# Row maxima gathered early, one weight's tiles spread over a stage, VectorE work queued behind the maxima

## The chip, the cores and the metric

The kernel runs on one core of one Trainium2 chip. The core has a matrix engine (TensorE, PE in the profile), VectorE (DVE), ScalarE (ACT), GpSimd (POOL) and DMA queues, here all issued by SyncE (SP). Each engine works through its own instruction queue in order; semaphores hold an instruction back until what it needs is there. The metric is the device time of one execution in microseconds, the median of several runs.

## The reference

Three blocks in a row, on 2 batches of 448 tokens with 768 channels:

```python
x = attention(q, k, v)                       # 12 heads of 64, causal
# mixer: over tokens, then over channels
h = np.maximum(x.transpose(0, 2, 1) @ w_tok1, 0.0) @ w_tok2
u = x + h.transpose(0, 2, 1)
y = u + np.maximum(u @ w_ch1, 0.0) @ w_ch2   # 768 -> 1536 -> 768
# gated block
h = gelu_tanh(y @ w_in)                      # 768 -> 2 x 512
a, v = h[..., :512], h[..., 512:]
v_n = (v - mean(v)) / np.sqrt(var(v) + 1e-06) * g_ln
v_s = np.einsum('ts,bsd->btd', w_sg, v_n) + b_sg[None, :, None]
out = y + (a * v_s) @ w_out                  # 512 -> 768
```

Inputs are float32 but the weights come as 64-bit words and are turned into float32 on the chip.

## The kernel before

Everything is kept with channels on the partitions (128 rows) and tokens along the row. After attention and the token mixer come these stages, named by their PSUM tiles:

- r (`channel_up`): u times `w_ch1` in 12 tiles of 128 channels.
- y (`channel_down`): 12 tiles `y_ps`, six channel tiles `m` by two batches `b`, 36 matmuls each. Each `m` needs two tiles of `w_ch2` of 128x768, one for each half of the contraction.
- v: seven token tiles `v_ps` of y times the second half of `w_in` (`w_inv`, in `wv32`), 18 matmuls each; token tile 3 has tokens of both batches and reads them from `y3`, into which POOL copies 64 columns of each y tile.
- ug: y times the first half of `w_in` (`w_inu`, four tiles of 128x768), then g (the mixing of tokens with `w_sg`, and the product `ug`), then o (twelve tiles times `w_out`, added to y by the `ob` instruction and written out).

A weight tile takes the same way everywhere (`decode`): SP loads 768 KB of raw words into `wraw` (two buffers), ACT turns the high words into a float (L117), DVE shifts (L120) and joins in the low words (L121). For the y stage `load_w` then splits it into two float32r parts: ACT casts `whi` (L130), POOL subtracts `wlo` (L99), three buffers each. For v, ug, g and o the operands are split into two float16 parts, scaled by the largest value of the tile. That maximum is found in steps: `absmax` makes row maxima (`yam`, `wvam`, `wam`, `gtam`), a reduction makes one column of them, PE spreads this column over all partitions with a matmul against the identity (`ys_ps`, `w_ps`, `gt_ps`), DVE reduces the result and takes the reciprocal (`spread`), and `split16` makes the high part on ACT and the low part on DVE (`y16`, `wl`). `to16` does it for y of one batch, `begin16` and `end16` for a tile of `w_inu` or `w_out`, `gate16` for the product.

The code states what depends on what. In which order the instructions stand in each engine's queue is set by a scheduler that simulates the program with its own costs; `tc.issue_after(x)` tells it to put instructions behind x.

Of the kernel before, what the change touches and what calls it, by code (L numbers as in the profile page):

```python
# [9 lines left out]
BF16 = mybir.dt.bfloat16  # L10
F16 = mybir.dt.float16
F32 = mybir.dt.float32
# [3 lines left out]
ALU = mybir.AluOpType  # L16
# [8 lines left out]
TOP = 32768.0  # L25
# [3 lines left out]
def mixer_kernel(  # L29
# [37 lines left out]

    const = ctx.enter_context(tc.tile_pool(name="const", bufs=1))
    wpool = ctx.enter_context(tc.tile_pool(name="wpool", bufs=2))
    stp16 = ctx.enter_context(tc.tile_pool(name="stp16", bufs=2))  # L70
    sc = ctx.enter_context(tc.tile_pool(name="sc", bufs=1))
    upool = ctx.enter_context(tc.tile_pool(name="upool", bufs=1))
    rs = ExitStack()
# [66 lines left out]

    def absmax(dst, src):

        nc.vector.tensor_reduce(dst, src, AX.XY if len(src.shape) == 3 else AX.X, ALU.max, apply_absolute_value=True)

    def spread(pm, cols, inv, s, top):

        am = stp16.tile([P, 1], BF16, tag="am16", name="am16")
        nc.vector.tensor_reduce(am, cols, AX.X, ALU.max)
        nc.tensor.matmul(pm[:, :P], am.to_broadcast([P, P]), ident_b, start=True, stop=True)
        nc.vector.reduce_max(inv, pm[:, :P], axis=AX.X)  # L150
        nc.vector.tensor_scalar(inv, inv, 1e-20, 1.0 / top, ALU.max, ALU.mult)
        nc.vector.reciprocal(s, inv)
# [44 lines left out]
    def channel_up(m, batches, pool, psum):  # L197

        wh, wl = load_w(w_ch1[m])
        for b in batches:  # L200
# [6 lines left out]
            nc.vector.scalar_tensor_tensor(rl, pr[:, :S], 0.0, f32(rh), ALU.max, ALU.subtract)  # L207
            r_of[m, b] = (rh, rl)

    def channel_down(m, ws, batches, psum, tmp):  # L210

        for b in batches:
            py = psum.tile([P, 512], F32, tag="d", name="y_ps")
            mm3(py[:, :S], [((ws[c // NCC][0][:, c % NCC, :], ws[c // NCC][1][:, c % NCC, :]), r_of[c, b]) for c in range(NFF)])
            t = tmp.tile([P, S], F32, tag="yt", name="yt")
            nc.vector.tensor_add(t, py[:, :S], f32(u_hi[m][b]))  # L216
            y32[m][b] = upool.tile([P, S], F32, tag=f"uh{m}_{b}", name=f"y{m}_{b}")
            nc.gpsimd.tensor_add(y32[m][b], t, f32(u_lo[m][b]))  # L218
            absmax(yam[:, b, m:m + 1], y32[m][b])

    with ExitStack() as at:
        tokw = at.enter_context(tc.tile_pool(name="tokw", bufs=1))
# [280 lines left out]
    with rs:  # L503
        ps_d = ctx.enter_context(tc.tile_pool(name="ps_d", bufs=8, space=PSUM, reuse_waits="tile"))
        r1pool = rs.enter_context(tc.tile_pool(name="r1pool", bufs=1, reuse_waits="tile"))
        tmp = rs.enter_context(tc.tile_pool(name="tmp", bufs=3, reuse_waits="tile"))
        for m in range(NFF):
            channel_up(m, [1] if m < NF0 else [0, 1], r1pool, ps_d)
        def pst(name):
            return ps_d.tile([P, 512], F32, tag="d", name=name)  # L510

        def to16(b):

            spread(pst("ys_ps"), yam[:, b], *ysc[b], TOP)
            nc.vector.tensor_mul(vinv[:, 2 * b:2 * b + 1], ysc[b][0], wvsc[0])
            hs = slice(64 * b, 64 * b + 64)
            nc.vector.tensor_copy(vinv[hs, 1:2], vinv[hs, 2 * b:2 * b + 1])
            for m in range(NCC):
                y16[m][b] = upool.tile([P, 2, S], F16, tag=f"ul{m}_{b}", name=f"y16_{m}_{b}")
                split16(y16[m][b][:, 0], y16[m][b][:, 1], y32[m][b], ysc[b][1][:, 0:1])  # L520
                ts = slice((1 - b) * (S - 64), (1 - b) * (S - 64) + 64)
                nc.gpsimd.tensor_copy(y3[:, :, m, 64 * b:64 * b + 64], y16[m][b][:, :, ts])

        ws = {}
        for m in range(NCC):
            ws[m] = [
                load_w(w_ch2[m, :, c:c + NCC, :], **(dict(pool=tmp, bufs=1) if (m, c) == (NCC - 1, NCC) else {}))
                for c in (0, NCC)
            ]
            channel_down(m, ws[m], range(B) if m < NCC - 2 else [0], ps_d, tmp)  # L530
            for c in range(2 * m, 2 * m + 2) if m < NCC // 2 else ():
                decode(wv32[:, c, :], w_inv[:, c, :])
                absmax(wvam[:, c:c + 1], wv32[:, c, :])
            if m == NCC // 2:
                spread(pst("wv_ps"), wvam, *wvsc, TOP)
            for c in range(2 * m - NCC, 2 * m - NCC + 2) if m >= NCC // 2 else ():
                split16(wvh[:, c, :], wvl[:, c, :], wv32[:, c, :], wvsc[1][:, 0:1])
        channel_down(NCC - 2, ws[NCC - 2], [1], ps_d, tmp)
        to16(0)
        channel_down(NCC - 1, ws[NCC - 1], [1], ps_d, tmp)  # L540

    def ytok(i, c, vt):
        o = vt * P - S if vt > 3 else vt * P
# [28 lines left out]
    def begin16(src, j):  # L572

        k = src.shape[1]
        m = wpool.tile([P, WC], F32, tag="wm", name="wm", bufs=3)[:, :k * P]
        decode(m, src.rearrange("p a f -> p (a f)"))
        am = gw.tile([P, 1], F32, tag="wam", name="wam")
        absmax(am, m)
        begun.append((j, k, m, am))

# [10 lines left out]
    for vt in range(NV):  # L591
        if vt == 1:
            to16(1)
        if vt > 2:
            end16()
        if 2 <= vt <= 5:
            begin16(w_inu[vt - 2], vt - 2)
        pv = pst("v_ps")
        mm3(pv, [((ytok(0, c, vt), ytok(1, c, vt)), (wvh[:, c, :], wvl[:, c, :])) for c in range(NCC)])
        vg = gw.tile([P, DH], F32, tag="vg", name="vg")  # L600
        si = 0 if vt < 3 else 1 if vt == 3 else 2
        nc.scalar.activation(vg, pv, AF.Gelu_apprx_tanh, scale=vinv[:, si:si + 1])
        st = gw.tile([P, 6], F32, tag="st", name="st")
        nc.vector.bn_stats(st, vg)
        nc.vector.bn_aggr(mv[:, vt, :], st)
        rs = gw.tile([P, 1], F32, tag="rs", name="rs")
        nc.vector.tensor_scalar(rs, mv[:, vt, 1:2], 1.0e-6, ZSCALE ** -2, ALU.add, ALU.mult)
        nc.gpsimd.tensor_tensor(rs, rs, nhalf, ALU.pow)
        nc.vector.tensor_scalar(vg, vg, mv[:, vt, 0:1], rs[:, 0:1], ALU.subtract, ALU.mult)
        if vt != 3:  # L610
            nc.gpsimd.tensor_scalar(z_hi[:, vt, :], vg, 1.0, 0.0, ALU.mult, ALU.add)
            nc.gpsimd.tensor_sub(z_lo[:, vt, :], vg, z_hi[:, vt, :])
            continue
        for b in range(B):
            hs, ls = (slice(64 * i, 64 * i + 64) for i in (b, 1 - b))
            nc.scalar.copy(zz[b][hs], vg[hs])
            nc.gpsimd.tensor_sub(zz[b][ls], vg[hs], zz[b][hs])
# [33 lines left out]
    def gate16(b):  # L651

        us = slice(b * S, (b + 1) * S)
        spread(pst("gt_ps"), gtam[:, b], *gtsc[b], TOP)
        nc.vector.tensor_scalar(oinv[:, b], winv[:, NDC:], gtsc[b][0][:, 0:1], None, ALU.mult)
        for m in range(NDC):
            split16(gt_hi[:, m, us], gt_lo[:, m, us], ug[:, m, us], gtsc[b][1][:, 0:1])

    for b in range(B):
        us = slice(b * S, (b + 1) * S)  # L660
        for m in range(NDC):
            if b == 0 and m < 2:
                end16()
            if b == 1 and m == 2:
                gate16(0)
            ds_ = slice(m * P, (m + 1) * P)
            pg = pst("g_ps")
            nc.tensor.matmul(pg[:, :S], zz[b][:, ds_], sgh[:, 3, :], start=True, stop=False)
            nc.tensor.matmul(pg[:, :S], zz[b][:, ds_], sgl[:, 3, :], start=False, stop=False)
            vts_ = [c + 4 * b for c in range(3)]  # L670
            mm3(pg[:, :S], [((z_hi[:, vt, ds_], z_lo[:, vt, ds_]), (sgh[:, c, :], sgl[:, c, :])) for c, vt in enumerate(vts_)], True)
            gt = gw.tile([P, S], F32, tag="gt", name="gt")
            nc.vector.scalar_tensor_tensor(gt, pg[:, :S], gcol[:, m:m + 1], bb, ALU.mult, ALU.add)
            for cs, ts in rotated(b):
                nc.vector.tensor_mul(ug[:, m, cs], gt[:, ts], ug[:, m, cs])
            absmax(gtam[:, b, m:m + 1], ug[:, m, us])
    for b in range(B):
        us = slice(b * S, (b + 1) * S)
        for m in range(NCC):
            wh, wl = w16[NDC + m]  # L680
            if b == 0 and m == 2:
                gate16(1)
            ob = gw.tile([P, S], F32, tag="ob", name="ob")
            po = pst("o_ps")
            mm3(po[:, :S], [((wh[:, c, :], wl[:, c, :]), (gt_hi[:, c, us], gt_lo[:, c, us])) for c in range(NDC)])
            nc.vector.scalar_tensor_tensor(ob, po[:, :S], oinv[:, b, m:m + 1], y32[m][b], ALU.mult, ALU.add)
            nc.sync.dma_start(out[b, m], ob)


# [51 lines left out]
```

## Time and profile before

| | |
|---|---|
| runs | 427.32, 428.35, 430.29 us, median 428.35 |
| profiled execution | 431.07 us |
| its span | 429.3 us (1.8 us lie around it) |
| TensorE busy | 396.7 us (92%) |
| VectorE busy | 281.1 us (65%) |
| GpSimd busy | 205.1 us (48%) |
| ScalarE busy | 204.2 us (48%) |
| TensorE waits behind 196 us | 2.6 for `y_ps`, 1.3 for `ys_ps`, 1.4 for `w_ps`, 1.6 for `gt_ps` |

The rows below are read so: a timeline gives the start of an instruction in us from the span's start, its duration, engine, line, operation, what it writes and reads, and in brackets how long the engine had been idle before it and what released it. An instruction's duration reaches a little into the next one's. With xN, N instructions that followed each other stand in one row. A table of windows gives the busy time of each engine in a stretch, the clock granted to TensorE as a part of full speed, and the busy share of the DMA engines.

### The profile page before, as it was taken

What the parts mean: (1) busy time and instruction counts of PE and PEld (TensorE: products, weight loads), DVE (VectorE), ACT (ScalarE), POOL (GpSimd) and SP (SyncE); (2) the same over time, 40 slices, a digit from 0 to 9 for tenths busy, and PEclk for the clock granted to TensorE, in tenths of its full rate; (3) what the DMA queues carried; (4) which work ended last, traced back from release to release, by engine and by line L of the source; (5) the groups of instructions that cost most, each with busy time, mean ns of one, the idle gap of its engine ahead of it and who ended that gap; (6) DMA issues with size and microseconds to landing.
All of it is one profiled execution on the core that took longest, in us unless ns stands there. A gap on an engine that the chain in (4) does not pass through costs nothing.

```text
span 429.3 us, 7145 instructions
## 1 busy us (share of the span) xinstructions
PE 396.7 (92%) x2602; PEld 304.8 (71%) x2602; DVE 281.1 (65%) x661; ACT 204.2 (48%) x384; POOL 205.1 (48%) x205
## 2 busy tenths in 40 slices
PE   5778899796899999999999979999998989999896
PEld 3445687674688999999999969999983435555453
DVE  4979665799735745454545363359568999679822
ACT  3789767578866454454344222234143544432200
POOL 3686847678877572655124066364243847100000
PEclk9999899999999999999999989999999999999999
DMA  7899878999955835455536443344122022100122
GB/s 212 186 291 244 184 131 181 241 261 283 237 131 125 199 121 171 143 204 168 159 121 206 152 151 101 120 147 144 53 32 78 0 99 98 49 2 0 66 105 87
DMA packets 61458, 60.98 MB, mean 142 GB/s; under 512 B 47856, under 2 KB 53104, under 8 KB 61424
## 3 DMA queue, kind: packets, MB, share of 16 engines
q1 hardware_dynamic: 61424, 60.54, 52.2%
q8 instruction: 20, 0.33, 0.3%
q14 instruction: 14, 0.11, 0.1%
HBM read 46.50 MB, written 2.75 MB: 115 GB/s over the span
## 4 chain that ended last, share of the span: by engine, by line
PE 49%; DMA 17%; DVE 12%; issue 7%; POOL 7%; ACT 5%; SPq 3%; POOLq 0%; ACTq 0%; DVEq 0%
DMA wraw<-in 8%; PE y_ps L165 5%; PE y_ps L163 5%; PE y_ps L164 5%; DMA vr<-in 4%; PE r_ps L165 4%; PE r_ps L164 4%; PE r_ps L163 4%; DMA pT<-hl 3%; POOL wlo L99 2%; PE ug_ps L163 2%; PE ug_ps L164 2%; PE ug_ps L165 2%; PE o_ps L163 2%; PE o_ps L165 2%
## 5 line engine op out<-in xcount | busy, mean ns | idle before, releaser
L99 POOL TENSOR_TENSOR wlo<-wm,whi 128x768 fp32r<-128x768 f32 x31 | 66.3, 2138 | 57.6 <-ACT whi L130 55.1
L117 ACT ACTIVATE wm<-wraw 128x768 f32<-128x768 f32 (+2 forms) x47 | 38.8, 825 | 64.8 <-POOL wlo L99 45.5
L338 POOL TENSOR_TENSOR hl<-pe,hl 128x512 f16<-128x512 f32 x43 | 54.6, 1277 | 26.4 <-ACT hl L337 25.0
L311 PE MATMUL s_ps<-k,q 128*128 128x64 f32 (+3 forms) x216 | 55.0, 393 | 9.2 <-DMA q<-in 4.4
L120 DVE TENSOR_SCALAR wm<-wm 128x768 int32<-128x768 int32 (+2 forms) x47 | 28.3, 602 | 42.2 <-ACT wm L117 42.2
L165 PE MATMUL y_ps<-rh,wlo 128*128 128x448 f32 x144 | 53.4, 371 | 2.6 <-POOL wlo L99 2.6
L121 DVE SCALAR_TENSOR_TENSOR wm<-wraw,wm 128x768 int32<-128x768 int32 (+2 forms) x47 | 52.9, 1126 | 0.8
L163 PE MATMUL y_ps<-rh,whi 128*128 128x448 f32 x144 | 53.4, 371 | 0.0
L164 PE MATMUL y_ps<-rl,whi 128*128 128x448 f32 x144 | 53.2, 370 | 0.0
L163 PE MATMUL r_ps<-uh,whi 128*128 128x448 f32 x144 | 53.1, 369 | 0.0
L164 PE MATMUL r_ps<-ul,whi 128*128 128x448 f32 x144 | 53.1, 368 | 0.0
L165 PE MATMUL r_ps<-uh,wlo 128*128 128x448 f32 x144 | 52.7, 366 | 0.0
L311 PEld LDWEIGHTS s_ps<-k,q 128*128 128x128 f32 x216 | 30.3, 199 | 19.7 <-DVE mx L316 4.4
L316 DVE CUSTOM_DVE_ANT_0 pe<-s_ps,mask 128x192 f32<-128x192 f32 (+3 forms) x84 | 34.9, 443 | 4.5 <-PE s_ps L311 4.4
L325 ACT ACTIVATE pe<-pe,bias 128x448 f32<-128x448 f32 (+3 forms) x74 | 35.3, 527 | 0.3
L130 ACT CAST whi<-wm 128x768 fp32r<-128x768 f32 x31 | 25.7, 828 | 18.3 <-PE y_ps L164 8.7
L218 POOL TENSOR_TENSOR y<-yt,ul 128x448 f32<-128x448 f32 x12 | 14.9, 1244 | 40.7 <-DVE yt L216 34.0
L362 PE MATMUL x_ps<-vh,pT 128*128 128x65 f16 (+1 forms) x240 | 25.9, 197 | 7.3 <-DMA pT<-hl 6.5
L362 PEld LDWEIGHTS <-pT 128*128 128x128 f16 (+1 forms) x240 | 21.1, 98 | 14.4 <-DMA pT<-hl 9.6
L165 PEld LDWEIGHTS y_ps<-rh,wlo 128*128 128x128 f32 x144 | 27.5, 191 | 5.2 <-POOL wlo L99 3.0
L337 ACT CAST hl<-pe 128x512 f16<-128x512 f32 x43 | 26.2, 612 | 8.3 <-DMA pT<-hl 8.2
L163 PEld LDWEIGHTS y_ps<-rh,whi 128*128 128x128 f32 x144 | 27.5, 191 | 2.2
(176 smaller groups left out, 936.4 us busy)
## 6 DMA issues: line engine op xcount, KB each, us to landing
wraw<-in SPq DMA_DIRECT2D x35, 768.0 KB, 4.4
wraw<-in SPq DMA_DIRECT2D x14, 512.0 KB, 3.7
vr<-in SPq DMA_DIRECT2D x12, 320.0 KB, 4.6
k<-in SPq DMA_DIRECT2D x12, 224.0 KB, 3.6
q<-in SPq DMA_DIRECT2D x24, 112.0 KB, 3.8
out<-ob SPq DMA_DIRECT2D x12, 224.0 KB, 1.9
wraw<-in SPq DMA_DIRECT2D x3, 256.0 KB, 3.0
pT<-hl SPq DMA_TRANSPOSE x43, 4.0
```

The source lines that it names most:

```text
L99: nc.gpsimd.tensor_sub(lo, src, f32(hi))
L117: nc.scalar.activation(m, words.bitcast(F32)[:, :, 1], AF.Prelu, scale=2.0 ** -112, alpha=-(2.0 ** 32))
L120: nc.vector.tensor_scalar(mi, mi, 3, None, ALU.logical_shift_left)
L121: nc.vector.scalar_tensor_tensor(mi, words[:, :, 0], 29, mi, ALU.logical_shift_right, ALU.bitwise_or)
L163: nc.tensor.matmul(ps, lh, rh, start=i == 0 and not begun, stop=False)
L164: nc.tensor.matmul(ps, lh, rl, start=False, stop=False)
L165: nc.tensor.matmul(ps, ll, rh, start=False, stop=i == n - 1)
L311: nc.tensor.matmul(ps[:, o:o + m], qp[:, q0:q0 + P], k2[:, ks], start=True, stop=True)
L316: nc.vector.tensor_tensor_reduce(out=pe[:, cs], in0=ps[:, cs], in1=mask0 if i == 0 else mask[:, MASKS[i]], scale=-1.0 / math.sqrt(D), scal ...
L325: nc.scalar.activation(pe[:, cs], pe[:, cs], AF.Exp, bias=bias[:, j:j + 1], scale=-1.0)
L338: nc.gpsimd.tensor_sub(hl[:, 1], pe, hl[:, 0])
L362: nc.tensor.matmul(o, ph, vh[:, c, h, :D + 1], start=j == 0, stop=False)
```

## The change

- `spread` gets the gathered column instead of making it. A new `top_of` makes it, once each for y of each batch, for `w_inv` and for the product of each batch; for a `w_inu` or `w_out` tile `absmax` writes the column in bfloat16 at once, so ten small reductions go away.
- The `w_inv` tiles were decoded two each for the first three `m`; now one each for `m` 0 to 3 and two for `m` 4. Their spreading and splitting comes behind the loop.
- `begin16` of a `w_inu` tile and the `ob` instructions of the o stage are issued behind the last `top_of` of y and of the product. (The first concerns DVE's instructions of `begin16`: DMA and ACT's step are not held back by it.)
- `stp16` has one buffer of each name.

```diff
--- before.py
+++ after.py
@@ -67,7 +67,7 @@
 
     const = ctx.enter_context(tc.tile_pool(name="const", bufs=1))
     wpool = ctx.enter_context(tc.tile_pool(name="wpool", bufs=2))
-    stp16 = ctx.enter_context(tc.tile_pool(name="stp16", bufs=2))
+    stp16 = ctx.enter_context(tc.tile_pool(name="stp16", bufs=1))
     sc = ctx.enter_context(tc.tile_pool(name="sc", bufs=1))
     upool = ctx.enter_context(tc.tile_pool(name="upool", bufs=1))
     rs = ExitStack()
@@ -140,12 +140,18 @@
 
     def absmax(dst, src):
 
-        nc.vector.tensor_reduce(dst, src, AX.XY if len(src.shape) == 3 else AX.X, ALU.max, apply_absolute_value=True)
-
-    def spread(pm, cols, inv, s, top):
-
-        am = stp16.tile([P, 1], BF16, tag="am16", name="am16")
-        nc.vector.tensor_reduce(am, cols, AX.X, ALU.max)
+        return nc.vector.tensor_reduce(dst, src, AX.X, ALU.max, apply_absolute_value=True)
+
+    def top_of(cols, name):
+
+        am = stp16.tile([P, 1], BF16, name=name)
+        last_top[0] = nc.vector.tensor_reduce(am, cols, AX.X, ALU.max).ins
+        return am
+
+    last_top = [None]
+
+    def spread(pm, am, inv, s, top):
+
         nc.tensor.matmul(pm[:, :P], am.to_broadcast([P, P]), ident_b, start=True, stop=True)
         nc.vector.reduce_max(inv, pm[:, :P], axis=AX.X)
         nc.vector.tensor_scalar(inv, inv, 1e-20, 1.0 / top, ALU.max, ALU.mult)
...
+    yam16, gtam16 = {}, {}
+
...
             y32[m][b] = upool.tile([P, S], F32, tag=f"uh{m}_{b}", name=f"y{m}_{b}")
             nc.gpsimd.tensor_add(y32[m][b], t, f32(u_lo[m][b]))
             absmax(yam[:, b, m:m + 1], y32[m][b])
+            if m == NCC - 1:
+                yam16[b] = top_of(yam[:, b], f"yam16_{b}")
 
     with ExitStack() as at:
         tokw = at.enter_context(tc.tile_pool(name="tokw", bufs=1))
@@ -511,7 +521,7 @@
 
         def to16(b):
 
-            spread(pst("ys_ps"), yam[:, b], *ysc[b], TOP)
+            spread(pst("ys_ps"), yam16[b], *ysc[b], TOP)
             nc.vector.tensor_mul(vinv[:, 2 * b:2 * b + 1], ysc[b][0], wvsc[0])
             hs = slice(64 * b, 64 * b + 64)
             nc.vector.tensor_copy(vinv[hs, 1:2], vinv[hs, 2 * b:2 * b + 1])
@@ -528,16 +538,18 @@
                 for c in (0, NCC)
             ]
             channel_down(m, ws[m], range(B) if m < NCC - 2 else [0], ps_d, tmp)
-            for c in range(2 * m, 2 * m + 2) if m < NCC // 2 else ():
+            for c in ([m], [m], [m], [m], [m, m + 1], [])[m]:
                 decode(wv32[:, c, :], w_inv[:, c, :])
                 absmax(wvam[:, c:c + 1], wv32[:, c, :])
-            if m == NCC // 2:
-                spread(pst("wv_ps"), wvam, *wvsc, TOP)
-            for c in range(2 * m - NCC, 2 * m - NCC + 2) if m >= NCC // 2 else ():
-                split16(wvh[:, c, :], wvl[:, c, :], wv32[:, c, :], wvsc[1][:, 0:1])
+            if m == NCC - 2:
+                wvam16 = top_of(wvam, "wvam16")
+        spread(pst("wv_ps"), wvam16, *wvsc, TOP)
+        for c in range(NCC):
+            split16(wvh[:, c, :], wvl[:, c, :], wv32[:, c, :], wvsc[1][:, 0:1])
         channel_down(NCC - 2, ws[NCC - 2], [1], ps_d, tmp)
         to16(0)
         channel_down(NCC - 1, ws[NCC - 1], [1], ps_d, tmp)
+        last_y = last_top[0]
 
     def ytok(i, c, vt):
         o = vt * P - S if vt > 3 else vt * P
@@ -574,7 +586,7 @@
         k = src.shape[1]
         m = wpool.tile([P, WC], F32, tag="wm", name="wm", bufs=3)[:, :k * P]
         decode(m, src.rearrange("p a f -> p (a f)"))
-        am = gw.tile([P, 1], F32, tag="wam", name="wam")
+        am = gw.tile([P, 1], BF16, tag="wam", name="wam")
         absmax(am, m)
         begun.append((j, k, m, am))
 
@@ -594,7 +606,8 @@
         if vt > 2:
             end16()
         if 2 <= vt <= 5:
-            begin16(w_inu[vt - 2], vt - 2)
+            with tc.issue_after(last_y):
+                begin16(w_inu[vt - 2], vt - 2)
         pv = pst("v_ps")
         mm3(pv, [((ytok(0, c, vt), ytok(1, c, vt)), (wvh[:, c, :], wvl[:, c, :])) for c in range(NCC)])
         vg = gw.tile([P, DH], F32, tag="vg", name="vg")
@@ -651,7 +664,7 @@
     def gate16(b):
 
         us = slice(b * S, (b + 1) * S)
-        spread(pst("gt_ps"), gtam[:, b], *gtsc[b], TOP)
+        spread(pst("gt_ps"), gtam16[b], *gtsc[b], TOP)
         nc.vector.tensor_scalar(oinv[:, b], winv[:, NDC:], gtsc[b][0][:, 0:1], None, ALU.mult)
         for m in range(NDC):
             split16(gt_hi[:, m, us], gt_lo[:, m, us], ug[:, m, us], gtsc[b][1][:, 0:1])
@@ -674,6 +687,8 @@
             for cs, ts in rotated(b):
                 nc.vector.tensor_mul(ug[:, m, cs], gt[:, ts], ug[:, m, cs])
             absmax(gtam[:, b, m:m + 1], ug[:, m, us])
+        gtam16[b] = top_of(gtam[:, b], f"gtam16_{b}")
+    last_gt = last_top[0]
     for b in range(B):
         us = slice(b * S, (b + 1) * S)
         for m in range(NCC):
@@ -683,7 +698,8 @@
             ob = gw.tile([P, S], F32, tag="ob", name="ob")
             po = pst("o_ps")
             mm3(po[:, :S], [((wh[:, c, :], wl[:, c, :]), (gt_hi[:, c, us], gt_lo[:, c, us])) for c in range(NDC)])
-            nc.vector.scalar_tensor_tensor(ob, po[:, :S], oinv[:, b, m:m + 1], y32[m][b], ALU.mult, ALU.add)
+            with tc.issue_after(last_gt):
+                nc.vector.scalar_tensor_tensor(ob, po[:, :S], oinv[:, b, m:m + 1], y32[m][b], ALU.mult, ALU.add)
             nc.sync.dma_start(out[b, m], ob)
 
 
```

What this does to the queues, at three places. First ACT's queue in the y stage, around the casts of the third and fourth `w_ch2` tile (in the first piece `whi_3250` and `whi_3260`, in the second `whi_3244` and `whi_3254`; `wv32` are `w_inv` tiles). Before:

```order
L206 ACTIVATE rh_3107<-r_ps_3088 128x448
L130 CAST whi_3250<-wm_3252 128x768
L206 ACTIVATE rh_3130<-r_ps_3111 128x448
L117 ACTIVATE wv32_2592<-wraw_3470 128x512
L117 ACTIVATE wm_3378<-wraw_3379 128x768
L117 ACTIVATE wv32_2592<-wraw_3476 128x512
L130 CAST whi_3260<-wm_3262 128x768
```

After:

```order
L212 ACTIVATE rh_3107<-r_ps_3088 128x448
L130 CAST whi_3244<-wm_3246 128x768
L212 ACTIVATE rh_3130<-r_ps_3111 128x448
L117 ACTIVATE wv32_2592<-wraw_3458 128x512
L117 ACTIVATE wm_3366<-wraw_3367 128x768
L130 CAST whi_3254<-wm_3256 128x768
```

The cast of the fourth tile stands behind one `wv32` tile, the ninth load of the stage, where it stood behind two, the eleventh and twelfth.

Second, DVE's queue from the last row maximum of y on (`y5_1`), where the v stage begins. Before, with the first y16 of the second batch as the twelfth instruction behind the last row shown:

```order
L143 TENSOR_REDUCE yam_2596<-y5_1_3843 128x1
L143 TENSOR_REDUCE wam_3975<-wm_3969 128x1
L143 TENSOR_REDUCE wam_4024<-wm_4018 128x1
L143 TENSOR_REDUCE wam_4075<-wm_4069 128x1
L148 TENSOR_REDUCE am16_3907<-yam_2596 128x1
L148 TENSOR_REDUCE am16_4008<-wam_3975 128x1
```

After, the beginning, and then, behind five rows left out, the rest up to that y16:

```order
L143 TENSOR_REDUCE yam_2596<-y5_1_3843 128x1
L148 TENSOR_REDUCE yam16_1_3846<-yam_2596 128x1
L120 TENSOR_SCALAR wm_3969<-wm_3969 128x768
L120 TENSOR_SCALAR wm_4016<-wm_4016 128x768
L121 SCALAR_TENSOR_TENSOR wm_3969<-wraw_3970,wm_3969 128x768
L121 SCALAR_TENSOR_TENSOR wm_4016<-wraw_4017,wm_4016 128x768
L156 TENSOR_REDUCE yinv1_2600<-ys_ps_3908 128x1
L634 TENSOR_REDUCE sg_am_4189<-sgr_3862 128x1
```

```order
L618 BN_AGGR mv_3877<-st_3899 128x2
L120 TENSOR_SCALAR wm_4065<-wm_4065 128x768
L158 RECIPROCAL ys1_2601<-yinv1_2600 128x1
L525 TENSOR_TENSOR vinv_2611<-yinv1_2600,wvinv_2602 128x1
L618 BN_AGGR mv_3877<-st_3960 128x2
L620 TENSOR_SCALAR rs_3902<-mv_3877 128x1
L121 SCALAR_TENSOR_TENSOR wm_4065<-wraw_4066,wm_4065 128x768
L527 COPY vinv_2611<-vinv_2611 64x1
L620 TENSOR_SCALAR rs_3963<-mv_3877 128x1
L156 TENSOR_REDUCE winv_2609<-w_ps_4007 128x1
L163 SCALAR_TENSOR_TENSOR y16_0_1_3915<-y0_1_3235,ys1_2601,y16_0_1_3915 128x448
```

The gathered maximum comes directly behind the last row maximum, and the L120 and L121 of three `w_inu` tiles now stand between it and the first y16. Farther on, the decoding of the fourth `w_inu` tile (`wm_4112`) stands among the low parts of the others, up to its row maximum:

```order
L622 TENSOR_SCALAR vg_3996<-vg_3996,mv_3877,rs_4001 128x512
L120 TENSOR_SCALAR wm_4112<-wm_4112 128x768
L163 SCALAR_TENSOR_TENSOR wl1_4062<-wm_4016,wsc_2610,wh1_4061 128x768
L121 SCALAR_TENSOR_TENSOR wm_4112<-wraw_4113,wm_4112 128x768
L163 SCALAR_TENSOR_TENSOR wl2_4109<-wm_4065,wsc_2610,wh2_4108 128x768
L120 TENSOR_SCALAR wm_4205<-wm_4205 128x512
L143 TENSOR_REDUCE wam_4118<-wm_4112 128x1
```

The fourth `w_ps` waits for this row maximum, which now comes behind one more low part than before.

Third, DVE's queue at the beginning of the o stage. Before:

```order
L675 TENSOR_TENSOR ug_3859<-gt_4644,ug_3859 128x384
L686 SCALAR_TENSOR_TENSOR ob_4649<-o_ps_4650,oinv_2613,y0_0_3193 128x448
L143 TENSOR_REDUCE gtam_2608<-ug_3859 128x1
L686 SCALAR_TENSOR_TENSOR ob_4665<-o_ps_4666,oinv_2613,y1_0_3309 128x448
L148 TENSOR_REDUCE am16_4682<-gtam_2608 128x1
```

After:

```order
L688 TENSOR_TENSOR ug_3861<-gt_4624,ug_3861 128x384
L143 TENSOR_REDUCE gtam_2608<-ug_3861 128x1
L148 TENSOR_REDUCE gtam16_1_4629<-gtam_2608 128x1
L702 SCALAR_TENSOR_TENSOR ob_4631<-o_ps_4632,oinv_2613,y0_0_3193 128x448
L702 SCALAR_TENSOR_TENSOR ob_4647<-o_ps_4648,oinv_2613,y1_0_3303 128x448
```

The gathered maximum of the product has moved ahead of the two `ob` instructions. On SP's queue the loads follow the new order of the `w_inv` tiles, and the loads of the small arrays (`bb`, `sgr`, `gcol`) stand between the second and third `w_inu` tile; before they stood behind all four and the first `w_out` tile.

## Rows read from the trace of the kernel before

**Rows 1.** Timeline of TensorE in the y stage

```profile
247.56 0.37 PE L164 MATMUL y_ps<-rl,whi 128*128 128x448 f32 x1
250.55 0.47 PE L165 MATMUL y_ps<-rh,wlo 128*128 128x448 f32 x1 [2.62 <-POOL wlo L99]
...
254.84 0.36 PE L163 MATMUL y_ps<-rh,whi 128*128 128x448 f32 x1
```

**Rows 2.** Windows: length, busy PE PEld DVE ACT POOL, clock, DMA share, GB/s

```profile
252.00:254.00 2.00, 2.00 (x7) 1.79 (x6) 1.51 (x3) 0.15 (x1) 1.72 (x1) 0.50 0.00 0
346.00:350.00 4.00, 2.59 (x14) 1.04 (x13) 3.67 (x16) 0.48 (x1) 0.56 (x2) 1.00 0.65 231
```

**Rows 3.** Timeline of TensorE in the v stage

```profile
326.75 0.23 PE L149 MATMUL ys_ps<-ident_b,am 128*128 128x128 bf16 x1 [1.33 <-DVE am L148]
...
334.58 0.22 PE L149 MATMUL w_ps<-ident_b,am 128*128 128x128 bf16 x1
...
347.98 0.23 PE L149 MATMUL w_ps<-ident_b,am 128*128 128x128 bf16 x1 [1.41 <-DVE am L148]
```

**Rows 4.** Timeline of TensorE at the start of the o stage

```profile
402.56 0.23 PE L149 MATMUL gt_ps<-ident_b,am 128*128 128x128 bf16 x1 [1.59 <-DVE am L148]
```

**Rows 5.** Timeline of GpSimd, y stage and v stage

```profile
248.69 1.80 POOL L99 TENSOR_TENSOR wlo<-wm,whi 128x768 fp32r<-128x768 f32 x1
...
332.10 0.67 POOL L522 COPY y<-y 128x128 f16<-128x128 f16 x1
...
343.12 1.34 POOL L612 TENSOR_TENSOR z_lo<-vg,z_hi 128x512 f16<-128x512 f32 x1
```

**Rows 6.** Timeline of ScalarE in the y stage

```profile
231.29 0.89 ACT L117 ACTIVATE wm<-wraw 128x768 f32<-128x768 f32 x1 [1.77 <-POOL wlo L99]
...
245.49 0.66 ACT L117 ACTIVATE wv<-wraw 128x512 f32<-128x512 f32 x1 [5.93 <-DMA wraw<-in]
246.05 0.82 ACT L130 CAST whi<-wm 128x768 fp32r<-128x768 f32 x1
...
267.59 0.89 ACT L117 ACTIVATE wm<-wraw 128x768 f32<-128x768 f32 x1 [4.02 <-POOL wlo L99]
```

**Rows 7.** Timeline of VectorE at the start of the o stage

```profile
400.63 0.68 DVE L686 SCALAR_TENSOR_TENSOR ob<-o_ps,oinv,y 128x448 f32<-128x448 f32 x1 [0.50 <-PE o_ps L165]
401.23 0.61 DVE L143 TENSOR_REDUCE gtam<-ug 128x1 f32<-128x448 f32 x1
```

**Rows 8.** Timeline of VectorE at the start of the v stage

```profile
323.96 2.66 DVE L143 TENSOR_REDUCE wam<-wm 128x1 f32<-128x768 f32 x3
...
326.66 2.01 DVE L621 TENSOR_REDUCE sg_am<-sgr 128x1 bf16<-128x1792 f32 x1
328.59 0.68 DVE L604 BATCH_NORM_STATS2 st<-vg 128x6 f32<-128x512 f32 x1
...
329.72 0.15 DVE L152 RECIPROCAL ys<-yinv 128x1 f32<-128x1 f32 x1
...
330.99 5.01 DVE L157 SCALAR_TENSOR_TENSOR y<-y,ys,y 128x448 f16<-128x448 f32 x6
```

**Rows 9.** Timeline of VectorE: decoding and low parts, r stage and v stage

```profile
207.43 0.55 DVE L120 TENSOR_SCALAR wm<-wm 128x768 int32<-128x768 int32 x1
...
217.13 0.95 DVE L121 SCALAR_TENSOR_TENSOR wm<-wraw,wm 128x768 int32<-128x768 int32 x1
...
338.96 1.01 DVE L157 SCALAR_TENSOR_TENSOR wl<-wm,wsc,wh 128x768 f16<-128x768 f32 x1
...
340.65 1.90 DVE L157 SCALAR_TENSOR_TENSOR wl<-wm,wsc,wh 128x768 f16<-128x768 f32 x1
342.48 0.97 DVE L120 TENSOR_SCALAR wm<-wm 128x768 int32<-128x768 int32 x1
343.48 1.79 DVE L121 SCALAR_TENSOR_TENSOR wm<-wraw,wm 128x768 int32<-128x768 int32 x1
```

**Rows 10.** Loads into tile `wraw` from 205 to 345 us, issue to landing

```profile
DMA to landing us min/median/max: 3.5/4.2/5.9
```

## The prediction, made before the change was run

> **What bounds the kernel now.** I read the table first: TensorE (PE) is the one engine that is nearly always busy, so a change is worth what it takes from PE's idle time or adds to it, and nothing else counts until it makes PE wait. Then I looked for the rows of PE's timeline that carry a wait. Behind 196 us there are four, and the change touches the neighbourhood of each. The large one is in the y stage: the third matmul of a y tile starts at 250.55, after 2.62 us for a `wlo` from GpSimd (POOL) [rows 1]. It costs more than the wait itself: right behind it the granted clock is 0.50 [rows 2] and matmuls come every 0.37 us where they came every 0.20. From 247.56 to 254.84 there are 14 matmul intervals; at 0.203 each they would take 2.84 us, and they take 7.28. So this place costs 4.4 us, of which 1.8 is the clock. The three others are one short wait each for a reduction on VectorE (DVE): 1.33 us before `ys_ps`, 1.41 before the fourth `w_ps` [rows 3], 1.59 before the second `gt_ps` [rows 4]. Around the second of these the granted clock stays at 1.00 [rows 2], so I take all three at their own length.
>
> **The y stage: minus 4.4 us.** The `wlo` that PE waits for is subtracted from 248.69 [rows 5], behind ScalarE's cast of that tile (246.05 to 246.9). The cast itself stands behind the first step of a `wv32` tile, which waited 5.93 us for its DMA and began at 245.49 [rows 6]. That is the whole chain: a weight tile that PE needs at 247.8 is cast behind a transfer of a tile that nobody needs yet. In the new order one `w_inv` tile stands between two pairs of `w_ch2` tiles in place of two, and the cast stands directly behind the ninth load of the stage, which in the trace had landed by 231.29 [rows 6]. What the cast then waits for is its `whi` buffer, free when PE has read the tile of three before; that is half a y tile pair earlier, some 39 matmuls before 247.56, or 239.7. Cast 0.82 and subtraction 1.80 bring the tile to about 243.3 even with 1 us for queueing, over 4 us before its turn at 247.8. With no wait there is nothing behind which the clock falls. What is next late? The two extra `w_inv` tiles of the fifth round now come ahead of the cast of the eighth tile; its turn comes four y tiles of 36 matmuls behind that of the fourth, at 247.8 + 144 x 0.203 = 277.0, so with a first step, a cast and a subtraction (3.5 us) behind it the last of the two would have to land after about 273.5 to matter. The fifteenth and sixteenth loads were in by 262 to 268 [rows 6]. I charge nothing there, with the price of a failure among the rivals.
>
> **The end: minus 1.6 us.** Before, DVE does an `ob` that waits 0.50 us for its o tile (from 400.63), then the last `gtam`, then another `ob`, and only then the reduction that PE waits for until 402.56 [rows 4, 7]. Now the `ob` instructions stand behind that reduction. The `gtam` (0.61) can follow the last `ug` product at about 400.1, and the reduction (0.07) ends at about 400.8; PE reached the place at 402.56 - 1.59 = 400.97. The wait is gone. The two `ob` come some 0.7 us later than now, and what stands behind them is the next o tile's `ob` and output DMAs, twelve of which have more than 20 us to go; PSUM has eight buffers for them. Nothing added.
>
> **The v stage: plus 2.6 us, and a clock fall.** Here DVE work is taken out of the y stage and queued behind the last y maximum. `issue_after(last_y)` puts the L120 and L121 of the first three `w_inu` tiles behind it; before, they were done earlier, and what followed the maximum were only three `wam` (2.66 us together) and the rest of a shorter list [rows 8]. I sum DVE's new queue in steps from one start to the next (a duration less the 0.08 us by which the next starts early). It begins where the three `wam` began, 323.96. The gathered maximum 0.07 (so the `ys_ps` wait of 1.33 goes), two L120 at 0.47, two L121 at 0.87 [rows 9], the row maximum of `ys_ps` 0.2, `sg_am` 1.93, two `wam` at 0.86, two statistics at 0.60 and small ones of 0.07 [rows 8]: 332.0. Then the third tile's L120 0.47, L121 0.87 and nine small ones: 333.9, and only there the first low half of y16 of the second batch, 0.83 [rows 8]: 334.7. POOL's copy into `y3`, 0.64 [rows 5]: 335.3.
>
> PE, which no longer waits at `ys_ps`, is there at 325.42, and its next two v tiles take what they took, 326.75 to 334.58 = 7.83 us [rows 3]: it stands at the `y3` matmul at 333.25 and waits 2.05 us. From `ys_ps` to the fourth `w_ps` it had 19.82 us of work (326.75 to 347.98 - 1.41), so it reaches that `w_ps` at 325.42 + 19.82 + 2.05 = 347.3. A clock fall behind the first wait would be swallowed by the second.
>
> The third tile's wait on its DMA lies in the same queue, a new one: its `wraw` buffer is free when the first L121 is through, at 325.8, its transfer takes 4.2 us in the middle and 5.9 at most [rows 10], ScalarE's step 0.89 [rows 6]: 331.0, 1.0 us ahead of DVE's turn, at worst 0.7 late. Behind that instruction the whole y16 of the second batch is queued. I charge nothing and keep 0.7 for the range.
>
> DVE then goes on from 334.7: two scalings of a v tile (taken as L120's 0.47), a `wam` 0.86, five more y16 at 0.83: 340.6. Statistics and small ones 1.4: 342.0. `wl0` 0.93, small ones and POOL's power 1.0, a scaling 0.47: 344.4. Then L120, `wl1`, L121, `wl2`, a 512-wide L120 (0.33) and the fourth `wam` (0.86), which the fourth `w_ps` waits for. The four large ones cost 0.47, 0.93, 0.87, 0.93 by the quick rows and 0.97, 1.83, 1.72, 1.83 by the slow ones of the same shape [rows 9]; the slow rows lie beside POOL's z instructions (one at 343.12 [rows 5]). In the new order POOL has one such pair, some 2.7 us, to do there. I take the slow value for L120 and `wl1`, a third of the excess for `wl0`, the quick ones for the rest: 350.5, `w_ps` at 350.6. That is 2.6 us later than 347.98, and PE has waited 3.3.
>
> The Trainium skill, "SBUF — State Buffer", section "Who interferes with whom", holds that a VectorE instruction with two SBUF inputs and a GpSimd instruction that reads SBUF lock each other out for their whole length. The L121 of 343.48 agrees: POOL's `z_lo` ends at 344.46, 0.87 behind that is 345.3, and the row ends at 345.27 [rows 5, 9]. By that rule as much as POOL's whole pair could be lost, about 0.8 us more than I charge, and the time would be near 427.6.
>
> Behind a wait of 2.62 us the clock fell and cost 1.8; behind 1.41 it did not [rows 1, 2, 3]. A wait of 3.3 is nearer the first; I add 1.8.
>
> **Sum.** Against the profiled execution, 431.07 us (span 429.3 and 1.8 around it): -4.4 - 1.6 + 2.6 + 1.8 = -1.6, so 429.5. That execution is 0.63% above the median of the runs, 428.35; scaled by 428.35/431.07 the forecast is **426.8 us**. Ten removed reductions of 0.07 us on DVE lie beside PE work outside these places and give nothing.
>
> **Rivals.**
> *DVE keeps up.* The five y16 at 0.54 (the quick `wl` scaled to 448 columns) and all four large ones quick: the fourth `w_ps` at 347.5, PE there at 347.3. Then the v stage gives 0.5 and no clock falls: -6.5, so 421.9. For it: POOL has less beside DVE there than before. Against it: six y16 in a row took 0.83 each in the trace.
> *DVE is slow all through.* `wl0` and the four large ones at the slow rows: 352.9, the fourth `w_ps` 5.0 later, with the clock: +0.8, so 429.1. A third tile that lands late, 0.7, leads the same way. For it: three of the four such instructions from 338.96 on were slow [rows 9]. Against it: only one pair of z instructions is left there.
> *The y wait moves on instead of going.* The eighth `w_ch2` tile's cast now stands behind two `w_inv` tiles. If the second of these lands later than 273.5, PE waits for `wlo` there as it did at 250.55, at the same 4.4 us: -1.6 + 4.4 = +2.8, so 431.1, slower than before. Against it: 5 us of slack by the landed loads.
>
> **How the numbers follow.** Forecast 0.5 (425.0 without the clock fall to 427.9), DVE keeps up 0.23, DVE slow 0.12, the wait moves on 0.08, something else 0.07. From the bounds the range goes from the first rival, 421.7, to just short of the third, 430.6. A measurement here tells about 1% from no change, that is 424.1 and 432.6: faster gets the first rival and a little of the forecast, 0.25; slower the rest of the unexplained and a piece of the last, 0.07; the same 0.68.
>
> **What would show it.** In the profile after: no wait on `wlo` near 250 and a granted clock of 1.00 there; no wait at `ys_ps` and `gt_ps`; a wait of about 2 us at the first `y3` matmul and one of about 3 at the fourth `w_ps`, with 0.50 behind it; DVE without a gap from the last `yam` to there. If PE waits nowhere in the v stage, the DVE sum is wrong and the time is near 422; if a `wlo` wait shows up after 270, the third rival holds.

## The result, and the profile after

The changed kernel takes 430.64 us in the median (427.80 to 433.99, 20 runs), the kernel before 427.96 in as many (426.39 to 431.09): ratio 1.0063, interval 1.0038 to 1.0089. It is 2.7 us slower (1.6 to 3.8), where 426.8 was forecast. The profiled execution of it took 429.37 us, its span 427.6.

The table of TensorE's waits from 190 us to the end shows (total, times, longest) that three of the four old places are gone; the fourth, `w_ps`, costs 3.8 us where it cost 1.4, and one at `v_ps` is new:

```profile
PE w_ps L155 <- DVE wam L143: 3.8, 1, 3.8
PE v_ps L169 <- POOL y L532: 2.2, 1, 2.2
```

There is nothing on `wlo`, nothing at `ys_ps`, nothing at `gt_ps`. In the y stage, ScalarE's cast of the fourth tile waits for its buffer only, and GpSimd is through with the tile at 241.3; PE's turn is about 246.3 (92 matmuls at 0.2053 behind 227.4):

```profile
238.52 0.83 ACT L130 CAST whi<-wm 128x768 fp32r<-128x768 f32 x1 [6.30 <-PE y_ps L170]
```

```profile
239.49 1.85 POOL L99 TENSOR_TENSOR wlo<-wm,whi 128x768 fp32r<-128x768 f32 x1 [2.60 <-ACT whi L130]
```

VectorE's timeline from the last maximum of y on is the queue that the prediction summed. To compare the two, take 5.05 us off the forecast's times, since the last `yam` starts at 318.37 where it started at 323.42. Before:

```profile
323.42 0.62 DVE L143 TENSOR_REDUCE yam<-y 128x1 f32<-128x448 f32 x1 [1.24 <-POOL y L218]
```

After:

```profile
318.37 0.62 DVE L143 TENSOR_REDUCE yam<-y 128x1 f32<-128x448 f32 x1 [1.23 <-POOL y L226]
319.02 0.16 DVE L148 TENSOR_REDUCE yam<-yam 128x1 bf16<-128x6 f32 x1
319.10 1.02 DVE L120 TENSOR_SCALAR wm<-wm 128x768 int32<-128x768 int32 x2
320.03 1.82 DVE L121 SCALAR_TENSOR_TENSOR wm<-wraw,wm 128x768 int32<-128x768 int32 x2
...
326.95 0.53 DVE L120 TENSOR_SCALAR wm<-wm 128x768 int32<-128x768 int32 x1
...
327.65 0.95 DVE L121 SCALAR_TENSOR_TENSOR wm<-wraw,wm 128x768 int32<-128x768 int32 x1
...
329.09 0.67 DVE L163 SCALAR_TENSOR_TENSOR y<-y,ys,y 128x448 f16<-128x448 f32 x1
...
332.89 3.78 DVE L163 SCALAR_TENSOR_TENSOR y<-y,ys,y 128x448 f16<-128x448 f32 x4
...
340.84 1.29 DVE L163 SCALAR_TENSOR_TENSOR wl<-wm,wsc,wh 128x768 f16<-128x768 f32 x1
342.05 1.91 DVE L121 SCALAR_TENSOR_TENSOR wm<-wraw,wm 128x768 int32<-128x768 int32 x1
343.88 1.00 DVE L163 SCALAR_TENSOR_TENSOR wl<-wm,wsc,wh 128x768 f16<-128x768 f32 x1
...
345.14 0.94 DVE L143 TENSOR_REDUCE wam<-wm 128x1 bf16<-128x768 f32 x1
```

The first y16 comes 10.7 us behind the start of the `yam`. PE pays at the two places that the prediction named, and not at the `gt_ps` of [rows 4]:

```profile
330.43 0.39 PE L169 MATMUL v_ps<-wvh,y 128*128 128x512 f16 x1 [2.18 <-POOL y L532]
...
346.14 0.23 PE L155 MATMUL w_ps<-ident_b,wam 128*128 128x128 bf16 x1 [3.77 <-DVE wam L143]
...
400.86 0.23 PE L155 MATMUL gt_ps<-ident_b,gtam 128*128 128x128 bf16 x1
```

The row of the window around the second wait (columns as in [rows 2]) has the clock fall, to a mean of 0.72 of full speed over 5 us:

```profile
345.00:350.00 5.00, 3.86 (x13) 1.51 (x14) 5.00 (x12) 1.24 (x2) 0.00 (x0) 0.72 0.58 209
```

So what was foretold of the trace is there (VectorE's queue has one marked gap, of 0.32 us at 339.83), and the kernel is still slower instead of faster. One thing in the trace was not foretold. The view of the tile `y_ps` gives, for each line, the least, middle and greatest duration in ns and the first and last start. Of the kernel after:

```profile
L169 PE MATMUL y_ps<-rh,whi x144: 362/367/447, 227.4 to 315.7; 128*128 128x448 f32 x144
```

There is no wait in this stage, and yet from the first to the last of these starts the 429 intervals take 88.3 us, where at 0.2027 they would take 87.0. The distance of matmuls (the mean time from one start to the next) between 262 and 286 us is 0.2053 us; in the kernel before it was 0.2027 there. The r stage shows the same two numbers. Both stages use float32r operands.

### The profile page after: what moved, and what is told of

It reads as the page before. It is cut to its first block, busy times and chain, and to the rows that moved or that the text cites. A ratio compares the mean times of both kernels' runs of the same rounds, so it can differ in the third digit from the quotient of the medians.

```text
span 427.6 us, 7133 instructions
## 1 busy us (share of the span) xinstructions
PE 396.5 (93%) x2602; PEld 302.4 (71%) x2602; DVE 282.2 (66%) x651; ACT 204.8 (48%) x384; POOL 202.3 (47%) x205
## 4 chain that ended last, share of the span: by engine, by line
PE 63%; DVE 15%; DMA 9%; issue 4%; POOL 3%; ACT 3%; SPq 3%; POOLq 0%; ACTq 0%; DVEq 0%
PE y_ps L171 7%; PE y_ps L169 7%; PE y_ps L170 7%; PE r_ps L171 6%; PE r_ps L170 6%; PE r_ps L169 6%; DMA vr<-in 4%; DVE wm L121 3%; DVE pe L326 3%; PE o_ps L170 2%; PE o_ps L171 2%; PE ug_ps L170 2%; PE ug_ps L171 2%; PE o_ps L169 2%; PE ug_ps L169 2%
## 5 line engine op out<-in xcount | busy, mean ns | idle before, releaser
L99 POOL TENSOR_TENSOR wlo<-wm,whi 128x768 fp32r<-128x768 f32 x31 | 64.7, 2087 | 58.5 <-ACT whi L130 58.4
L121 DVE SCALAR_TENSOR_TENSOR wm<-wraw,wm 128x768 int32<-128x768 int32 (+2 forms) x47 | 52.5, 1119 | 0.7
L120 DVE TENSOR_SCALAR wm<-wm 128x768 int32<-128x768 int32 (+2 forms) x47 | 28.8, 616 | 36.1 <-ACT wm L117 36.1
L170 PEld LDWEIGHTS r_ps<-ul,whi 128*128 128x128 f32 x144 | 27.0, 188 | 2.8 <-issue 0.4
L171 PEld LDWEIGHTS r_ps<-uh,wlo 128*128 128x128 f32 x144 | 27.0, 188 | 2.7 <-issue 0.2
```

The lines of the kernel that those rows point to most:

```text
L99: nc.gpsimd.tensor_sub(lo, src, f32(hi))
L120: nc.vector.tensor_scalar(mi, mi, 3, None, ALU.logical_shift_left)
L121: nc.vector.scalar_tensor_tensor(mi, words[:, :, 0], 29, mi, ALU.logical_shift_right, ALU.bitwise_or)
L170: nc.tensor.matmul(ps, lh, rl, start=False, stop=False)
L171: nc.tensor.matmul(ps, ll, rh, start=False, stop=i == n - 1)
```

## The experiments

**What is the wait in the y stage worth?** The kernel before ran once more:

> The kernel before, unchanged, in one more execution. Theory A (the 4.4 us at 250 us in the shown execution, wait and clock, are not what a usual execution of the kernel before has, so removing them gives nearly nothing): the time is near the median of 428, PE waits less than 1 us for wlo in the y stage and the clock stays at 1.00 there. Rival B (the wait is there in every execution, the change does remove 4.4 us, and pays more than was summed elsewhere): a wait of 2 to 3 us for wlo near 250 with a clock of 0.50 behind it, also at 428.

It took 427.03 us, its span 425.2. The wait for `wlo` is there, shorter, and TensorE's row and the windows behind it show no clock fall:

```profile
248.04 0.47 PE L165 MATMUL y_ps<-rh,wlo 128*128 128x448 f32 x1 [1.90 <-POOL wlo L99]
```

```profile
248.00:250.00 2.00, 1.96 (x10) 1.84 (x11) 1.02 (x2) 1.62 (x2) 1.33 (x2) 1.00 0.41 169
250.00:252.00 2.00, 2.00 (x12) 1.85 (x11) 1.04 (x2) 0.00 (x0) 2.00 (x1) 1.00 0.41 46
```

Theory A in its strong form (seldom there) falls, and so does B's price of 4.4: here the place costs 2.2 us (from the first to the last `y_ps` start, 227.3 to 317.1, are 89.8 us, against 87.6 in the next kernel). That kernel is the one before with only the placement of the `w_inv` tiles:

```diff
-            for c in range(2 * m, 2 * m + 2) if m < NCC // 2 else ():
+            for c in ([m], [m], [m], [m], [m, m + 1], [])[m]:
                 decode(wv32[:, c, :], w_inv[:, c, :])
                 absmax(wvam[:, c:c + 1], wv32[:, c, :])
-            if m == NCC // 2:
-                spread(pst("wv_ps"), wvam, *wvsc, TOP)
...
+        spread(pst("wv_ps"), wvam, *wvsc, TOP)
+        for c in range(NCC):
+            split16(wvh[:, c, :], wvl[:, c, :], wv32[:, c, :], wvsc[1][:, 0:1])
```

> The kernel before with nothing but the w_inv tiles spread as in the change. Theory A: the same within 0.3%, since the wait it removes is seldom there. Rival B: about 4.4 us faster, ratio 0.990.

Ratio 0.9948 (0.9910 to 0.9986), 425.48 us: 2.2 us faster, between the two theories. Its y stage has no wait:

```profile
L163 PE MATMUL y_ps<-rh,whi x144: 362/365/449, 230.0 to 317.2; 128*128 128x448 f32 x144
```

**What does the work behind the maxima cost?** The changed kernel without one line, and itself again, measured side by side:

```diff
-            with tc.issue_after(last_y):
-                begin16(w_inu[vt - 2], vt - 2)
+            begin16(w_inu[vt - 2], vt - 2)
```

> The changed kernel without issue_after(last_y): the decoding of the w_inu tiles goes back ahead of the last maximum of y. Both theories: the waits at the first y3 matmul (2.2 us) and at the fourth w_ps (3.8 us) and the clock fall behind the latter shrink to one wait of 1 to 2 us with no clock fall, worth 4 to 5 us against the changed kernel. Theory A: 426.5, ratio to before 0.996 (the 1.6 us of the o stage are what is left). Rival B: 422, ratio 0.986.

> The changed kernel on the chip of this call, as a measure for the others. Theory A: ratio to before 1.006, with waits of about 2.2 and 3.8 us in the v stage. The fp32r matmuls of the r and y stages stood 0.2053 us apart in the profile of the changed kernel and 0.2027 in that of the kernel before: if that belongs to the execution or the chip and not to the kernel, it is equal to that of the other kernels of this call; if it belongs to the change, it is 0.205 here and 0.203 in the kernel before.

Without the line 0.9970 (0.9935 to 1.0005), 427.09 us; with it 1.0105 (1.0046 to 1.0164), 433.09. The line costs 1.35%, 5.8 us, in these runs. Without it, PE's waits from 196 us on are short ones:

```profile
PE ys_ps L155 <- DVE yam L148: 1.3, 1, 1.3
PE gt_ps L155 <- DVE gtam L148: 1.2, 2, 0.7
PE w_ps L155 <- DVE wam L143: 0.4, 1, 0.4
```

In the changed kernel's second profile the two waits are 2.2 and 2.1 us and the clock falls behind the first, not behind the second. Both kernels have the distance 0.2053 in the r and y stages, while `wv_only` and the repeated kernel before, measured beside them, have 0.2027. So it belongs to the program, and to a part of the change that `wv_only` lacks and `no_last_y` has.

**Why are the float32r matmuls slower?** The addresses in the built programs offer a reason. `stp16` held two buffers of 32 bytes before; it now holds five differently named vectors of 32 bytes, and all pools behind it (u, and in its place y; r; others) start 96 bytes further on, for u at 61,152 in place of 61,056. Two kernels with the order of the changed one had the vectors packed as columns of two tiles, which takes the 96 bytes back, and two kernels were the one before with 32 or 64 bytes put ahead of u (the second piece below is the one of 32 bytes):

```diff
+    tops = [stp16.tile([P, n], BF16, name=f"tops{n}") for n in (2, 3)]
...
-        am = stp16.tile([P, 1], BF16, name=name)
+        n, c = {"yam16_0": (0, 0), "yam16_1": (0, 1), "wvam16": (1, 0), "gtam16_0": (1, 1), "gtam16_1": (1, 2)}[name]
+        am = tops[n][:, c:c + 1]
```

```diff
     sc = ctx.enter_context(tc.tile_pool(name="sc", bufs=1))
+    pad = sc.tile([P, 8], F32, name="pad")
+    nc.vector.memset(pad, 0.0)
```

> The changed kernel with its five gathered vectors as columns of two small tiles, so that all tiles behind them in memory start where they did in the kernel before; the order on every engine is unchanged. Theory C (the change moves u, r and the float32r weights by 96 bytes, off a 64-byte boundary, and each float32r matmul of the r and y stages then takes 0.0026 us more, 864 of them, 2.2 us): pitch 0.2027 again, and about 2.2 us less than the changed kernel, ratio to before near 1.001 to 1.005. Rival D (the pitch follows from the order of instructions or from the new tiles' dependencies, not from addresses): pitch stays at 0.2053 and the ratio at 1.006 to 1.010.

> The changed kernel without issue_after(last_y) and with the vectors packed as in after_packed. Theory C: 2.2 us less than without the packing, 425, ratio 0.992; pitch 0.2027. Rival D: 427, ratio 0.997.

> The kernel before with a tile of 32 bytes put ahead of u in memory, nothing else (and one small memset at the start). Theory C: pitch 0.2053 in the r and y stages, 2.2 us slower, ratio 1.005. Rival D: pitch 0.2027, ratio 1.000.

> The kernel before with 64 bytes ahead of u. Theory C, if it is the 64-byte boundary that matters: pitch 0.2027 and ratio 1.000. If any shift changes it, 0.2053 and 1.005. The y wait for wlo near 250: 1.9 us and no clock fall in one execution of before, 2.6 us with one in another; a third look.

The distance of float32r matmuls, between 262 and 286 us, went with the shift in every case: 0.2027 in both packed kernels, 0.2067 at 32 bytes, 0.2000 at 64, 0.2053 at 96. That the place decides is theory C; its numbers for the two pads missed, since 0.2053 was expected at 32 bytes and 0.2027 or 0.2053 at 64, so it is not a matter of a 64-byte boundary alone. In the tile view of `y_ps` it is the middle duration and, where no wait lies between, the first and last start. The packed changed kernel, 87.2 us:

```profile
L172 PE MATMUL y_ps<-rh,whi x144: 362/365/450, 229.1 to 316.3; 128*128 128x448 f32 x144
```

The kernel before with 32 bytes, 88.9 us:

```profile
L165 PE MATMUL y_ps<-rh,whi x144: 363/369/448, 229.4 to 318.3; 128*128 128x448 f32 x144
```

In time, packing gave 1.0026 (0.9988 to 1.0064) for the changed kernel, where it had 1.0063 and 1.0105, and 0.9915 (0.9881 to 0.9949) without the line on `last_y`, where it had 0.9970: 0.4 to 0.8% and 0.55%, where the 864 matmuls of the two stages at 0.00265 us each make 2.3 us, 0.5%. These ratios come from different sets of runs and their intervals overlap, so the times only fit the sum; what is shown directly is the distance in the traces, and by it rival D falls. For the kernel before with 32 bytes theory C foretold a slower kernel and missed: 0.9953 (0.9917 to 0.9988). Its matmuls are slower, as said, but its trace has no wait for `wlo`, although the `w_inv` tiles stand in the old places: the tile is done at 248.30, just ahead of PE's turn.

```profile
246.46 1.84 POOL L101 TENSOR_TENSOR wlo<-wm,whi 128x768 fp32r<-128x768 f32 x1
248.38 0.45 PE L167 MATMUL y_ps<-rh,wlo 128*128 128x448 f32 x1
```

Counted from the first `y_ps` start the tile is done after 18.9 us, where `before_again` had it after 20.7; PE's turn comes 0.35 us later than there. The r stage ahead of it is 1.7 us longer (432 x 0.004), which would give the transfers this lead; that it does is argued, not shown. With 64 bytes, 0.9963 (0.9923 to 1.0004), PE is earlier at the tile, and waits 2.58 us, with the clock at 0.50 behind it:

```profile
247.45 0.47 PE L167 MATMUL y_ps<-rh,wlo 128*128 128x448 f32 x1 [2.58 <-POOL wlo L101]
```

What PE gains ahead of that transfer it loses, in this trace, at the wait. Why the 32 bytes end up faster than the kernel before, and not even with it, is not settled.

**The parts again, at equal addresses.** Four more kernels were run side by side: the changed one, packed, with the old places of the `w_inv` tiles; one, packed, in which only the row maxima of the `w_inu` tiles stand behind `last_y` (its edit is below); and the changed order and this one at 64 bytes (the vectors in four tiles):

```diff
-            with tc.issue_after(last_y):
-                begin16(w_inu[vt - 2], vt - 2)
+            begin16(w_inu[vt - 2], vt - 2, last_y)
...
-    def begin16(src, j):
+    def begin16(src, j, behind=None):
...
-        absmax(am, m)
+        with tc.issue_after(behind) if behind is not None else ExitStack():
+            absmax(am, m)
```

> The changed kernel, vectors packed, with the w_inv tiles placed as in the kernel before. Theory A as mended (the wait for wlo in the y stage is there in most executions of that placement and costs 2 to 4.5 us, by whether the clock falls behind it): the wait near 250 us is back, y stage 90 to 92 us long against 87.6, 2 to 4 us slower than after_packed, ratio 1.007 to 1.012. Rival: the same as after_packed.

> The changed kernel, vectors packed, with only the row maxima of the w_inu tiles behind the last maximum of y; their L120 and L121 are free to go earlier, as in the kernel before. Theory E (what costs in the v stage is the decoding, 4 us of L120 and L121 ahead of the first y16, not the place of the maxima): no wait at ys_ps, none at the first y3 matmul, one of at most 2 us at the fourth w_ps without a clock fall; ratio to before 0.989 to 0.992. Rival F (any DVE work queued behind the last maximum delays y16): a wait at the y3 matmul of more than 1 us, ratio 0.997 or more.

> The changed kernel with its vectors in four tiles, all behind them 64 bytes further than in the kernel before and 32 less than in the changed one; the order unchanged. Theory C as mended: pitch 0.2000, 4.6 us less than the changed kernel (864 x 0.0053), ratio near 0.997; the waits of the v stage stay at 2 to 4 us each. Otherwise the ratio is that of after_packed, 1.003.

> As amax_only with the vectors in four tiles, so that u, r and the rest lie 64 bytes further on. Theory C as mended (the pitch follows the place modulo 128 bytes: 0.2027 at 0, 0.2066 at 32, 0.2000 at 64, 0.2053 at 96): pitch 0.2000 and 2.3 us less than amax_only, ratio 0.984 to 0.987. If before_pad64 had its 0.2000 from something else, 0.2027 and the time of amax_only.

`old_wv_packed`: 1.0081 (1.0048 to 1.0115), 0.55% or 2.4 us above `after_packed`, which was measured at another time; the two intervals overlap a little. The wait is back, with no clock fall, in a y stage of 89.1 us where 90 to 92 was expected:

```profile
249.69 0.47 PE L174 MATMUL y_ps<-rh,wlo 128*128 128x448 f32 x1 [1.24 <-POOL wlo L99]
```

`amax_only`: 0.9924 (0.9896 to 0.9953), at the edge of the 0.989 to 0.992 of theory E. No wait at `ys_ps`, none at `y3`, none at `gt_ps`; of PE's waits behind 196 us one is left, and the clock falls behind it here, which theory E had ruled out, but not in the kernel's copy at 64 bytes (the profile here is of the slowest of its eight executions, 428.53 us against a median of 425.02):

```profile
PE w_ps L158 <- DVE wam L143: 2.0, 1, 2.0
```

`after_64`: 0.9923 (0.9894 to 0.9953), 425.46 us, with two waits of 2.2 and 2.1 us as in `after_again`; it is faster than the distance alone explains (0.997 was expected), and why is open. `amax_only_64`: **0.9844 (0.9815 to 0.9873), 422.05 us**, faster than both kernels, with matmuls 0.2000 apart, 86.1 us in this row:

```profile
L172 PE MATMUL y_ps<-rh,whi x144: 362/363/451, 227.3 to 313.4; 128*128 128x448 f32 x144
```

Two comparisons here are between kernels measured side by side, with intervals that do not meet. `amax_only_64` is 0.8% faster than `after_64` at the same addresses, so it is the decoding behind `last_y` that costs, and rival F falls. It is 0.8% faster than `amax_only` with the same edit of the order, so the addresses alone are worth this much. That the row maxima gain anything behind `last_y` is not shown: with nothing behind it, `no_last_y_packed` had 0.9915 where `amax_only` has 0.9924.

## Why the prediction was wrong

Two steps of the sum failed, of about equal size: the first term was too large, and a term was missing.

**The y stage: minus 4.4 us.** The mechanism was right: the wait is gone in every profile with the `w_inv` tiles spread, and there in four of the five with the old places. The size was off. The 4.4 is what the place cost in the one execution whose profile was read; the spreading alone measured 2.2 us (0.6 to 3.9), its undoing 2.4. Against a y stage without the wait at the same distance of matmuls, the traces with the old places cost 1.5 and 2.2 us without a clock fall, 4.4 and 4.5 with one, and about nothing with 32 bytes (89.3 us, where 431 intervals of 0.2067 make 89.1). So the first step that failed is this term together with its scaling. The profiled execution of 431.07 us took 4.0 us more than the one of 427.03, of which 2.2 lie in the y stage and 1.8 ahead of it; a term read from it whole was then scaled by 0.63%, as if the excess were spread evenly.

**A term that the sum lacks: plus 2.3 us.** This is the second step that failed: a cost put at nothing without a reason. "Nothing added" was said of work; what the five vectors do to the addresses behind them was not considered, and the runs showed float32r matmuls 0.2053 us apart in place of 0.2027. No row of the trace of before could show the price, but that the addresses move could have been seen ahead.

**The v stage: plus 2.6 us, and a clock fall (1.8).** Right, place by place. Set back by the 5.05 us, the forecast had the first y16 at 328.85 (329.09 measured), a wait of 2.05 at `y3` (2.18), the fourth `w_ps` at 345.55 (346.14) behind a wait of 3.3 (3.77), then 0.50 of the clock. From the last `y_ps` matmul to the first `ug_ps` the kernel before takes 30.9 us, the changed one 35.7 in the first profile, 4.8 more where 4.4 was summed, and 34.1 in the second, where the clock fell behind the first wait and the second wait swallowed that, as was said. The line costs more than these 3.2 to 4.8 us when it is taken out, 5.8 and, with packing, 1.1% or 4.8. Without it the v stage takes 29.6 us, less than before, though PE waits at `ys_ps` as before.

That the sum came so close is in part luck: what the slow VectorE rows were charged at was about right in total, but for the wrong instructions. L120 and `wl1` were nearly quick (0.55, 1.29), L121 was slow (1.91), and a scaling (1.31) and the y16 (0.94 each) cost more than assumed. GpSimd's rows beside them, after, and the one beside the slow L120 of [rows 9], before:

```profile
340.46 0.86 POOL L624 TENSOR_SCALAR z_hi<-vg 128x512 f16<-128x512 f32 x1 [0.67 <-DVE vg L622]
341.40 1.73 POOL L625 TENSOR_TENSOR z_lo<-vg,z_hi 128x512 f16<-128x512 f32 x1
```

```profile
341.71 1.32 POOL L611 TENSOR_SCALAR z_hi<-vg 128x512 f16<-128x512 f32 x1
```

The L120 that took 0.97 began (342.48) while a `z_hi` was running; the one that took 0.55 began (340.29) before one. By the Trainium skill, "SBUF — State Buffer", section "Who interferes with whom", a VectorE instruction with two SBUF inputs, such as L121, contends with a GpSimd instruction that reads SBUF. The trace agrees again: `z_lo` ends at 343.13, 0.87 behind that is 344.0, and the row of L121 ends at 343.96. But the whole pair was not lost, as the larger estimate had it.

**The end: minus 1.6 us.** Right where no wait is left: from the first `ug_ps` to the end 77.3 us before, 75.8 after. In the second profile 0.5 of waiting stayed and it was 76.3. The size is 1.0 to 1.5.

**The rivals.** *DVE keeps up* did not hold, nor did *the y wait moves on*: no `y_ps` wait shows up in any profile with spread tiles. *DVE is slow all through* had the fourth `w_ps` at 347.9 (352.9 less 5.05); it came at 346.14. The forecast's sum with its two errors mended, the other terms as measured, reads: y stage -2.2, addresses +2.3, v stage +3.2 to +4.8, end -1.0 to -1.5, together +1.8 to +3.9; 2.7 was measured.

## What to carry to other kernels

A wait that is read from one execution has the price of that execution: where a transfer lands close to when it is needed and a clock fall hangs on the difference, read a second execution before it goes into a sum whole. Work that is queued behind a maximum to let the maximum out sooner stands ahead of everything that the maximum is for; move only the pieces that are short, and compare that with moving none. A handful of bytes allocated early shifts all that lies behind, so compare the addresses of matmul operands before and after, or pack small vectors into the tiles that were there.

## What was not expected of the hardware

The time of a 128x128 by 448 matmul in float32r goes with the place of its operands in memory: 0.2027 us from one to the next with u and r at the old addresses, 0.2067, 0.2000 and 0.2053 with them 32, 64 and 96 bytes further on, and programs of different order that share a place (at 0, 64 and 96 bytes there are two or more) share the number. The float16 matmuls of the o stage stand 0.189 us apart in both kernels, and with 32 and 64 bytes. The decoded weight buffers of these stages did not move, but for the last pair, so it is u and r, or how they lie to the weights; which, and whether it repeats every 128 bytes, was not tried.

From 190 us on, in the fourteen profiles, the granted clock stayed at 1.00 behind waits of 1.2 to 1.9 us and fell to 0.50 behind 2.6 and 3.8; behind 2.0 to 2.2 it fell in some executions and not in others.
